# A windowed-attention and feed-forward kernel whose instructions are put in order by another simulator of the framework

## The chip, the cores and the metric

One core of a Trainium2 chip runs the kernel. The metric is the device time of one execution in microseconds (us); lower is better. Several runs of one kernel are summed up by their median. Engines are named as in the profile: PE is TensorE (matrix multiplies), PEld its weight loads, DVE is VectorE, ACT is ScalarE, POOL is GpSimd, and SP is the queue from which this kernel issues its DMA transfers.

## The reference

Attention over 8 batches and 8 heads, with 512 local and 32 global tokens a head and a head width of 64. Global queries see every key; local queries see the global keys and a window of 32 positions to each side. The result, 4352 rows of 512, goes through a feed-forward that takes the maximum of three products:

```python
s_g = scale * np.matmul(q_g, k_all.transpose(0, 1, 3, 2))
out_g = np.matmul(sm(s_g), v_all)
s_ll = np.where(np.abs(pos[:, None] - pos[None, :]) <= 32, scale * np.matmul(q_l, k_l.transpose(0, 1, 3, 2)), -1e9)
s_lg = scale * np.matmul(q_l, k_g.transpose(0, 1, 3, 2))
a_l = sm(np.concatenate([s_lg, s_ll], axis=-1))
out_l = np.matmul(a_l, np.concatenate([v_g, v_l], axis=2))
...
x = np.ascontiguousarray(attn_out.transpose(0, 2, 1, 3)).reshape(B * S, H * D)
h = np.maximum(np.maximum(x @ w1, x @ w2), x @ w3)
return (h @ w_out).astype(np.float32)
```

Everything is float32. `sm` is a softmax.

## The kernel before

**The work and its tiles.** Two heads make a pair (`p`), four pairs a batch, so there are 32 pairs. A pair's 512 local queries are cut into 4 items of 128 queries (`t`), which makes 128 items (`sl`). An item's keys are 192 or 224 columns: its window and the 32 global ones. Most operands are split into a high part, rounded to fp32r, and a low part, the rest, so that a product is made of two or three fast matmuls. The split is a `copy` (L101, on DVE or ACT) and a `sub` (L94, on DVE or POOL). The first 28 items take plain float32 instead of split q and k.

**An item's chain.** `scores` (L324) multiplies q and k into a PSUM tile `S`. DVE scales, masks and takes the maximum (L354), ACT takes the exponential (L356), DVE sums and inverts (L358, L359), `times` (L109) scales `s`, on POOL (L120), DVE or ACT, and from item 16 on SP stores `s` into `prob` (L363). `trans` (L367) transposes it on PE into the PSUM tile `T` (L375), from which `pt` is split. `transg` (L386) transposes the global queries' probabilities (L393), which `glob` (L278) and `glob_soft` (L302) have made from one block of scores in each of a pair's first two items (L290, L294). `pv` (L403) multiplies `pt` by v into the PSUM tile `O` (L419, L426), and ACT and DVE add its parts into `xr`.

**The feed-forward as a filler.** `moe_group` (L449) is a generator that emits one matmul at a time (L465 for the three products, L484 for the second layer). `fill(n)` takes n of them, so that between the small matmuls of an item there are always some of the batch before. From item 16 on the counts are (4, 4, 3, 7). The first batch's feed-forward starts at item 8. The last batch's, and that of the global rows, have no attention beside them and run at the end. Evictions of their PSUM tiles are a `copy` and running maxima on DVE (L473); `h` and `xs` are split like the rest.

**The front.** 24 pieces of weights arrive as float32 and are rounded and split on ACT, POOL and DVE by hand (`convert`, L150), in steps that lie between the items of the first batch (`weight_step`, L189; the table `WS`, L512).

**What sets the order.** The Python code writes instructions down in one order, for all engines together:

```python
trans(sl + 1)
fill(n[0])
next_scores(sl + 4 if sl < 12 else max(15, sl + 3))
...
fill(n[1])
pv(sl)
...
fill(n[2])
transg(sl + 1)
fill(n[3])
split_v(sl + 2)
load_v(sl + 4)
```

`next_scores` calls `scores`, then `split_q` for the item after, then `load_q`. Which engine an operation goes to is decided there too, by a running sum of estimated costs (`least`, L84). When the `TileContext` is left, the framework orders each engine's instructions by executing the program on a simulated machine: among the instructions whose inputs and tiles are ready there, the one written first goes next. It gives out the buffers of each pool in the same pass and then sets the semaphores. On the chip, each engine's and each queue's instructions come in the order found.

## Time and profile before

| | |
|---|---|
| median of 3 runs | 837.66 us (835.61 to 838.0) |
| profiled execution | 835.65 us, span 833.5 us |
| PE busy | 807.3 us, 97% of the span |
| DVE, ACT, POOL busy | 522.6, 528.3, 513.9 us (63%, 63%, 62%) |
| DMA | 93.56 MB by SP's queue |
| mean granted PE clock | 0.993 of full speed |

The profiled execution's own time is 2.15 us longer than its span, and it is one of the quicker runs. A busy time is the union of an engine's instructions. Matmuls overlap in the pipeline and their ends are modelled, so a full stretch of PE says that it always had work, not that it ran at its peak. Engine busy shares are averages over stages with different limits, so they are read stage by stage below.

### The profile page before, as it was taken

What the parts mean: (1) busy time and instruction counts of PE and PEld (TensorE: products, weight loads), DVE (VectorE), ACT (ScalarE), POOL (GpSimd) and SP (SyncE); (2) the same over time, 40 slices, a digit from 0 to 9 for tenths busy, and PEclk for the clock granted to TensorE, in tenths of its full rate; (3) what the DMA queues carried; (4) which work ended last, traced back from release to release, by engine and by line L of the source; (5) the groups of instructions that cost most, each with busy time, mean ns of one, the idle gap of its engine ahead of it and who ended that gap; (6) DMA issues with size and microseconds to landing.
All of it is one profiled execution on the core that took longest, in us unless ns stands there. A gap on an engine that the chain in (4) does not pass through costs nothing.

```text
span 833.5 us, 15973 instructions
## 1 busy us (share of the span) xinstructions
PE 807.3 (97%) x4668; PEld 684.4 (82%) x4668; DVE 522.6 (63%) x1784; ACT 528.3 (63%) x1498; POOL 513.9 (62%) x727
## 2 busy tenths in 40 slices
PE   7789899899999999999999999999999999999997
PEld 5569788878888888888888888888888888888896
DVE  4778735867776767767676776777776776411111
ACT  6688756776776777777776677777677666411210
POOL 4789836886677667867676676866776664311211
PEclk9899999999999999999999999999999999999999
DMA  7567544443334333343335333443335331100001
GB/s 261 175 225 228 183 127 131 137 130 103 105 115 143 114 91 112 105 146 100 103 106 166 107 99 109 120 140 94 95 93 172 109 90 53 59 13 1 26 26 26
DMA packets 93414, 94.56 MB, mean 113 GB/s; under 512 B 18448, under 2 KB 81808, under 8 KB 93328
## 3 DMA queue, kind: packets, MB, share of 16 engines
q1 hardware_dynamic: 93328, 93.56, 36.3%
q8 instruction: 37, 0.61, 0.3%
q14 instruction: 49, 0.40, 0.2%
HBM read 56.85 MB, written 8.91 MB: 79 GB/s over the span
## 4 chain that ended last, share of the span: by engine, by line
PE 83%; DVE 1%; POOL 1%; issue 1%; ACT 1%; DMA 0%; POOLq 0%; DVEq 0%; ACTq 0%
PE pm L465 48%; PE pm L484 16%; PE O L426 6%; PE S L351 5%; PE T L375 4%; PE S L294 2%; PE S L393 1%; PE S L347 1%; PE O L419 1%; DMA prob<-s 0%; ACT s L356 0%; DVE kst L105 0%; POOL s L120 0%; DVE xr L434 0%; DVE sg L298 0%
## 5 line engine op out<-in xcount | busy, mean ns | idle before, releaser
L465 PE MATMUL pm<-xs,wh 128*128 128x512 f32 (+1 forms) x1440 | 422.0, 368 | 5.7 <-ACT xs L107 2.3
L465 PEld LDWEIGHTS pm<-xs,wh 128*128 128x128 f32 x1440 | 253.3, 189 | 36.4 <-ACT xs L107 2.7
L465 PE MATMUL pm<-xs,wl 128*128 128x512 f32 (+1 forms) x720 | 265.1, 368 | 0.2 <-POOL wl L173 0.2
L465 PEld LDWEIGHTS pm<-xs,wl 128*128 128x128 f32 x720 | 136.3, 189 | 20.6 <-issue 1.6
L120 POOL TENSOR_SCALAR s<-s,z 128x224 f32<-128x224 f32 (+1 forms) x246 | 104.9, 438 | 64.8 <-ACT lox L107 40.9
L484 PE MATMUL pm<-woh,h 128*128 128x512 f32 x408 | 133.4, 399 | 0.9 <-POOL h L99 0.9
L99 POOL TENSOR_TENSOR h<-m,h 128x512 fp32r<-128x512 f32 (+1 forms) x60 | 68.6, 1143 | 97.8 <-ACT h L107 97.6
L356 ACT ACTIVATE s<-s,nm 128x224 f32<-128x224 f32 (+1 forms) x256 | 118.1, 462 | 16.5 <-DVE nm L354 12.8
L473 DVE TENSOR_TENSOR m<-pm,m 128x512 f32<-128x512 f32 (+1 forms) x120 | 73.0, 608 | 72.1 <-PE pm L465 71.6
L99 POOL TENSOR_TENSOR qs<-qraw,qs 128x256 fp32r<-128x256 f32 x100 | 73.1, 739 | 62.5 <-ACT qs L107 54.2
L99 DVE TENSOR_TENSOR pt<-T,pt 128x512 fp32r<-128x512 f32 x102 | 70.5, 691 | 62.6 <-ACT pt L107 61.3
L354 DVE CUSTOM_DVE_ANT_0 s<-S,mask 128x224 f32<-128x224 f32 (+1 forms) x240 | 80.7, 371 | 24.5 <-PE S L347 18.0
L484 PEld LDWEIGHTS pm<-woh,h 128*128 128x128 f32 x408 | 74.6, 188 | 13.6 <-POOL h L99 1.5
L484 PE MATMUL pm<-wol,h 128*128 128x512 f32 x204 | 82.1, 403 | 1.2 <-POOL wol L173 1.2
L99 POOL TENSOR_TENSOR kst<-kraw,kst 64x576 fp32r<-64x576 f32 x50 | 71.6, 1432 | 12.9 <-issue 6.2
L99 POOL TENSOR_TENSOR vs<-vraw,vs 128x256 fp32r<-128x256 f32 x102 | 75.4, 740 | 6.3 <-ACT vs L107 3.0
L107 ACT CAST pt<-T 128x512 fp32r<-128x512 f32 x88 | 51.3, 583 | 40.4 <-PE T L375 40.4
L107 ACT CAST qs<-qraw 128x256 fp32r<-128x256 f32 x99 | 40.2, 407 | 53.9 <-PE S L351 50.3
L426 PEld LDWEIGHTS O<-pt,vs 128*128 128x128 f32 x408 | 66.1, 188 | 8.8
L426 PE MATMUL O<-pt,vs 128*128 128x320 f32 (+1 forms) x408 | 72.8, 300 | 0.0
L351 PEld LDWEIGHTS S<-kst,qs 128*128 128x128 f32 x400 | 59.6, 190 | 8.9 <-DVE nmg L298 0.6
L434 DVE TENSOR_TENSOR xr<-O,lox 64x160 f32<-64x160 f32 x204 | 64.3, 315 | 3.4
(97 smaller groups left out, 1222.6 us busy)
## 6 DMA issues: line engine op xcount, KB each, us to landing
vraw<-v_in SPq DMA_DIRECT2D x64, 256.0 KB, 3.1
qraw<-q_in SPq DMA_DIRECT2D x100, 128.0 KB, 2.2
prob<-s SPq DMA_DIRECT2D x56, 224.0 KB, 2.4
wraw<-w_in SPq DMA_DIRECT2D x24, 512.0 KB, 3.6
prob<-s SPq DMA_DIRECT2D x56, 192.0 KB, 2.3
out_dram<-o SPq DMA_DIRECT2D x32, 256.0 KB, 2.5
kraw<-k_in SPq DMA_DIRECT2D x25, 320.0 KB, 3.0
qn<-q_in SPq DMA_DIRECT2D x8, 256.0 KB, 5.6
```

The lines of the kernel that those rows point to most:

```text
L99: (dve if least(c) == "d" else pool).tensor_tensor(out=out, in0=a, in1=b, op=ALU.subtract)
L107: act.copy(out=out, in_=a)
L120: pool.tensor_scalar(out=out, in0=a, scalar1=col, scalar2=1.0, op0=ALU.mult, op1=ALU.mult)
L351: pe.matmul(ph[j][:, 0:n], lhsT=qs[i][:, a, 128 * j:128 * j + 128], rhs=kst[p][:, j, c0:c0 + n], start=(a == 0), stop=(a == 1))
L354: dve.tensor_tensor_reduce(out=s[:, j, 0:n], in0=ph[j][:, 0:n], in1=mask[:, (1, 0, 1, 0)[t], 32 * (t == 0):32 * (t == 0) + n], scale=-0.12 ...
L356: act.activation(out=s[:, j, 0:n], in_=s[:, j, 0:n], func=AF.Exp, bias=nm[:, j:j + 1], scale=-1.0, accum_out=ze[:, j, 0:1])
L375: pe.transpose(pr[:, 256 * j + 128 * c:256 * j + 128 * c + 128], s[:, j, 128 * c:128 * c + 128], one)
L426: pe.matmul(o[:, j, 0:320].rearrange("p (a q) -> p a q", a=2)[:, :, 0:n], lhsT=vs[sl][:, 2 * j + c].rearrange("p a d -> p (a d)"), rhs=pt[ ...
L434: dve.tensor_tensor(out=xr[p][64 * j:64 * j + 64, t], in0=o[0:64, j, 0:160], in1=lo[:, j], op=ALU.add)
L465: pe.matmul(ps[:, 0:n], lhsT=w[f][:, i, k], rhs=xs[k][:, a, c0:c0 + n], start=(q == 0), stop=(q == 11))
L473: dve.tensor_tensor(out=m[:, 0:n], in0=ps[:, 0:n], in1=m[:, 0:n], op=ALU.max)
L484: pe.matmul(ps, lhsT=hh[f][:, a, 128 * t:128 * t + 128], rhs=w[:, f], start=(q == 0), stop=(q == 17))
```

## The change

One argument: the context is told to order the instructions by the framework's timeline simulation instead of its core simulation. The kernel's body stays as it is, and with it every instruction, the engine that it runs on, and every tile and transfer. What may differ is the place of an instruction in its engine's queue, the buffer that a tile gets, and the waits that follow from both.

```diff
-    with tile.TileContext(nc) as tc:
+    with tile.TileContext(nc, schedule_with_timeline_sim=True) as tc:
```

## The prediction

> **What bounds the kernel now.** I read the page first, then the busy time by stretches, then what TensorE (PE) waited for, then the chain of work that ended last, and only then single instructions. From the page:
>
> ```profile
> span 833.5 us, 15973 instructions
> ...
> PE 807.3 (97%) x4668; PEld 684.4 (82%) x4668; DVE 522.6 (63%) x1784; ACT 528.3 (63%) x1498; POOL 513.9 (62%) x727
> ...
> PE   7789899899999999999999999999999999999997
> ...
> PEclk9899999999999999999999999999999999999999
> ```
>
> PE is busy nearly throughout; what it lacks lies in the first slices. The stretches show it in numbers (after each engine its busy us, then PE's granted clock, DMA share, GB/s):
>
> ```profile
> 0.00:180.00 180.00, 158.54 (x1097) 132.02 (x1098) 121.22 (x440) 127.26 (x379) 127.93 (x197) 0.97 0.57 180
> 180.00:720.00 540.00, 540.00 (x2990) 458.17 (x2990) 381.39 (x1306) 382.72 (x1084) 369.61 (x514) 1.00 0.36 111
> 720.00:833.50 113.50, 108.80 (x585) 94.22 (x583) 20.01 (x38) 18.30 (x37) 16.32 (x17) 0.99 0.06 21
> ```
>
> ```profile
> 0.00:20.00 20.00, 14.92 (x73) 10.36 (x74) 9.06 (x55) 12.37 (x40) 9.21 (x24) 1.00 0.78 262
> 20.00:60.00 40.00, 30.67 (x184) 22.09 (x183) 30.47 (x103) 30.01 (x89) 30.77 (x50) 0.87 0.61 195
> 60.00:100.00 40.00, 37.39 (x293) 33.65 (x292) 33.37 (x92) 32.33 (x88) 36.38 (x49) 1.00 0.68 216
> 100.00:140.00 40.00, 39.41 (x300) 33.80 (x299) 17.93 (x86) 23.28 (x76) 19.14 (x30) 1.00 0.46 139
> 140.00:180.00 40.00, 36.14 (x257) 32.12 (x256) 30.38 (x110) 29.28 (x89) 32.43 (x47) 1.00 0.43 127
> ```
>
> There are three stages. In the front (0 to 180 us) PE is idle 180 - 158.54 = 21.46 us, and between 20 and 100 us DVE, ACT and POOL are as loaded as it is: weights are converted there beside the attention of the first batch. In the middle (180 to 720 us) PE has no idle time and the full clock, while the other three are busy 382.72 us of 540 at most, 71%. The tail (from 720 us) is the feed-forward of the last batch and of the global rows, with the others nearly idle; its 4.7 us without PE lie at the very end. So PE's amount of work is the bound, and only the front's 21.46 us stand above it. What PE waited for, over the whole run:
>
> ```profile
> PE S L290 <- DMA qg<-k_in: 4.2, 1, 4.2
> PE S L393 <- POOL probg L120: 2.3, 1, 2.3
> PE pm L465 <- ACT xs L107: 2.3, 2, 1.5
> PE pm L465 <- POOL xs L99: 2.2, 2, 1.8
> PE T L375 <- DMA prob<-s: 1.4, 3, 0.8
> ```
>
> The first is the first load, which no order can shorten. The others are single waits of 0.8 to 2.3 us, on three different engines: no one resource holds the front.
>
> **The change part by part.** It adds and removes no instruction, tile or transfer. It changes which simulated machine decides, instruction by instruction, what each engine and the DMA queue is given next; the chip then takes each queue in that order. So the whole price is a price of order, stage by stage. First, how far does the present order already depart from the written one? PE, from the chain of waits:
>
> ```profile
> 402.50 0.29 PE T L375 x4
> 402.79 1.00 PE pm L465 x4
> 403.79 0.44 PE S L351 x4
> 404.23 0.94 PE pm L465 x4
> 405.16 0.58 PE O L426 x4
> 405.75 0.70 PE pm L465 x3
> 406.44 0.06 PE S L393
> 406.50 1.67 PE pm L465 x7
> ```
>
> That is the order in which the loop writes it: transposes, 4 feed-forward matmuls, scores, 4, PV, 3, the global transpose, 7, the (4, 4, 3, 7) of L558. Here the simulated order made no choice on PE. On POOL it did:
>
> ```profile
> 404.75 0.74 POOL L99 TENSOR_TENSOR qs<-qraw,qs 128x256 fp32r<-128x256 f32 x1 [2.45 <-ACT qs L107]
> 406.29 0.88 POOL L120 TENSOR_SCALAR s<-s,z 128x224 f32<-128x224 f32 x2 [0.80 <-ACT lox L107]
> 407.14 0.74 POOL L99 TENSOR_TENSOR vs<-vraw,vs 128x256 fp32r<-128x256 f32 x1
> ```
>
> The loop writes the scaling of s (in scores) before the split of the next q (split_q), and here the split goes first. So POOL, and by the same reasoning ACT, DVE and the queue of SP, are the ones to be reshuffled.
>
> Middle, 540 us: I cost it at 0. A gain is excluded: PE has no idle time there. What hides a reshuffle is the slack of the other engines. The tightest hand-over I find is the PSUM tile S, of which there are two: in an item with a global score block, the tile of S L351 has to be read by DVE before the global transpose (L393) can be given it, if the two take turns.
>
> ```profile
> 410.21 0.35 DVE L354 CUSTOM_DVE_ANT_0 s<-S,mask 128x192 f32<-128x192 f32 x1
> ```
>
> ```profile
> 412.24 0.22 PE L393 MATMUL S<-identr,probg 128*128 128x128 f32 x1
> ```
>
> DVE is done at 410.56, PE needs the tile at 412.24: 1.68 us of slack. The longest DVE operation that could step ahead is the running maximum:
>
> ```profile
> 404.89 0.69 DVE L473 TENSOR_TENSOR m<-pm,m 128x512 f32<-128x512 f32 x1
> ```
>
> Two of these (1.38 us) still fit; three (2.07 us) cost 0.39 us an item. That cover gone, over the 54 items behind the front that have such a block (t of 0 or 1, pairs 4 to 30), is 0.39 x 54 = 21 us: the upper end for this stage. Long waits elsewhere are no sign of danger:
>
> ```profile
> POOL h L99 <- ACT h L107: 97.6, 27, 18.4
> ...
> SPq L363 <- POOL s L120: 189.6, 74, 8.6
> ```
>
> The first row is POOL standing with h at the head of its queue. What is behind it there (scalings of s, splits of q and v) waits too, and PE does not notice. The second is SP standing with the store of s into prob, with the loads of q and v behind it; PE lost only the 1.4 us of its row above to that hand-over. If the new order puts a load of q ahead of a prob store, or the reverse, SP pays with time it has.
>
> Tail, 113.5 us: 0, since PE alone fills it, and 4.7 us are the last eviction and store.
>
> Front: this is where an order has something to win or lose. Upper end of a gain: 21.46 less the first load's 4.2, so 17 us, plus what the clock costs there. The granted clock by short stretches:
>
> ```profile
> 22.00:24.00 2.00, 0.26 (x1) 0.18 (x1) 1.97 (x5) 0.60 (x2) 1.82 (x5) 0.82 0.85 247
> 24.00:26.00 2.00, 2.00 (x9) 1.28 (x9) 0.52 (x4) 0.62 (x1) 1.82 (x6) 0.50 0.44 118
> 26.00:28.00 2.00, 2.00 (x14) 1.44 (x13) 1.95 (x7) 0.95 (x3) 1.16 (x1) 0.82 0.41 162
> ```
>
> A stretch with almost no matmul is followed by one at half the clock. It costs 2 x 0.50 + 2 x 0.18 = 1.4 us of PE; the mean of 0.87 over 20 to 60 us means 40 x 0.13 = 5 us in all. So the gain ends at 22 us. For a loss I take the same 22 us as the end, a front with twice the waits. Between these ends I stay near zero, nearest to the rows of single waits (0.8 to 2.3 us): a new order would remove some and make others. I lean to +1.5 us, less than one wait of 2.3, because the stretch with the most matmuls per us among the loaded ones, 60 to 100 us, has only 2.6 us of PE idle left to win and POOL busy 36.38 of 40 us: one operation in the wrong place there has nothing to hide behind.
>
> [...]
>
> Sum: 835.65 us is the time of the profiled execution (span 833.5 and 2.15 around it); + 0 (middle) + 0 (tail) + 1.5 (front) = 837.2. The median of the runs, 837.66, is 2.0 above the profiled one, so against it I say 839.
>
> **The rivals.**
> 1. The front gets better: the other machine places conversions, scalings and splits closer to when their inputs are really there, and a third to two thirds of the 22 us go, 7 to 15. For it: the PE waits there fall on single late operations (xs, probg), which one place earlier would cure. Against it: ACT, DVE and POOL are busy 75 to 91% between 20 and 100 us, so the room is small, and I take the lower half: 837.66 - 9 = 829, and 823 at the best.
> 2. The middle loses its cover: DVE or POOL is given the feed-forward's evictions ahead of the reading of S by three operations or more in every such item. For it: the period repeats, so that a bad place is paid 54 times. Against it: 29% of slack on each engine, and PE's own order has not moved at all there. Price as above: 837.66 + 21 = 859; it decides from 1.7 us of delay on.
> 3. The clock: the front's waits stay as long in sum but fall so that two or three more stretches run at half the clock, 3 x 1.4 = 4.2 us, with the 1.5 of the front 843 us. For it: three 2 us stretches of the kind above fit into the 5 us found. Against it: it can as well lose one.
> 4. Nothing moves that PE sees, because both machines find PE the bound: 837.7.
>
> **How the numbers follow.** A measurement of this kernel tells 0.3% from no change, 2.5 us: same is 835.1 to 840.2. My forecast (front shifted by a few us, middle untouched) has 0.50, with its own range 834 to 845: 0.08 of that is faster, 0.23 same, 0.19 slower. Rival 1 has 0.19, all faster; rival 2 0.18, slower; rival 3 0.05, slower; rival 4 0.08, same. Faster 0.08 + 0.19 = 0.27; same 0.23 + 0.08 = 0.31; slower 0.19 + 0.18 + 0.05 = 0.42. The range leaves out the better half of rival 1 (below 828) and the worse half of rival 2 (above 857, where the delay passes 1.68 us by more than 0.36 in each of 54 items): about 0.19 together.
>
> **What would show it.** Right: PE still fully busy from 180 to 720 us at the period of before, its idle time differing only ahead of 180 us, by under 5 us, and POOL's order of qs, s and vs changed. The middle's step is wrong if PE shows waits there at S (L393, L351) or T (L375), or if its row of items no longer reads T, 4, S, 4, O, 3, S, 7. The front's step is wrong if PE idles under 15 or over 28 us before 180 us. The whole is wrong if the new order moves PE itself: feed-forward matmuls pulled ahead in the front would then be missing as filler later, a cost that no row here prices.

## The result and the profile after

The changed kernel takes 894.89 us (median of 4 runs, 891.57 to 896.84) against 837.14 us for the one before: a ratio of 1.0696, 95% interval 1.0678 to 1.0714, so 7% slower. I had said 839 us, with 857 as the upper end. The profiled execution took 893.29 us, with a span of 891.5 us and a mean granted clock of 0.955. One execution among the experiments below (of frontload_spare) took 939.16 us at a mean granted clock of 0.849, and no comparison uses it.

The page of the changed kernel, its span, busy times, PE's busy tenths in 40 slices and its granted clock:

```profile
span 891.5 us, 15955 instructions
...
PE 833.7 (94%) x4668; PEld 710.1 (80%) x4668; DVE 501.6 (56%) x1784; ACT 521.3 (58%) x1498; POOL 513.8 (58%) x727
...
PE   7688999989998999989999999979998999979997
...
PEclk9979999999998899979999999979998899989999
```

PE has the same 4668 matmuls, yet is busy 26.4 us longer (833.7 against 807.3), and idle 57.8 us instead of 26.2 (span less busy): together the 58 us of longer span. The slices show where: there are dents at regular distances, a busy 7 or 8, most of them with a clock of 7 or 8. Before, both rows were flat there. The same stretches as in the prediction:

```profile
0.00:180.00 180.00, 154.93 (x1064) 130.09 (x1065) 116.56 (x415) 119.12 (x358) 121.98 (x188) 0.95 0.54 173
...
180.00:720.00 540.00, 518.53 (x2746) 442.26 (x2745) 333.23 (x1216) 351.57 (x1011) 347.91 (x483) 0.95 0.34 106
```

The front lost little: 25.1 us idle instead of 21.5. The middle, which had none, has 21.5 us of idle time, a clock of 0.95, and gets through 2746 matmuls where it had done 2990.

One dent in the busy time by 2 us (columns as before: PE, PEld, DVE, ACT, POOL, granted clock, DMA share, GB/s):

```profile
380.00:382.00 2.00, 1.88 (x16) 1.62 (x14) 1.02 (x4) 1.50 (x5) 1.09 (x3) 1.00 0.37 122
382.00:384.00 2.00, 0.83 (x7) 0.73 (x7) 2.00 (x9) 1.79 (x8) 1.55 (x3) 1.00 0.71 210
384.00:386.00 2.00, 1.31 (x9) 0.86 (x8) 1.31 (x8) 1.31 (x5) 1.28 (x3) 0.77 0.17 39
386.00:388.00 2.00, 1.37 (x6) 1.16 (x7) 1.72 (x6) 1.95 (x6) 1.75 (x4) 0.50 0.22 67
388.00:390.00 2.00, 2.00 (x9) 1.90 (x10) 1.25 (x7) 1.93 (x7) 1.85 (x3) 0.50 1.01 275
390.00:392.00 2.00, 0.90 (x6) 0.74 (x6) 1.82 (x7) 0.97 (x4) 1.90 (x3) 0.50 0.53 165
392.00:394.00 2.00, 2.00 (x10) 1.90 (x10) 2.00 (x7) 1.95 (x6) 2.00 (x4) 0.50 0.31 97
```

PE has some work in each 2 us, but too little in most, and from 386 to 394 us it runs at half the clock. The chain of the same place (start, us, what; the shorter pieces left out):

```profile
379.86 0.47 PE pm L465 x2
...
380.72 0.67 PE O L426 x4
...
383.11 0.80 DVE pt L99 x2
...
385.00 0.60 ACT s L356 x3
...
388.48 2.64 DMA qraw<-q_in
...
391.57 1.30 PE O L426 x4
392.87 0.80 PE S L351 x4
393.67 1.33 PE pm L465 x3
```

And a little later:

```profile
399.56 5.26 PE pm L465 x23
...
407.65 2.80 PE pm L465 x12
...
415.64 3.50 PE pm L465 x15
```

Read against the row of 4, 4, 3, 7 of before, this shows what was lost in the middle. From 380.3 to 393.7 us there is no feed-forward matmul (L465); the end of the chain walks through DVE, ACT, POOL and a load instead of through PE. Behind it the feed-forward matmuls come in packs of 23, 12 and 15. Counts of L465 and of the PV matmuls (L426; 4 to an item) in two stretches of one batch, before first:

```profile
300.00:336.00 36.00, 30.23 (x112) 19.26 (x112) 1.00 0.35 104
384.00:396.00 12.00, 9.90 (x38) 6.36 (x37) 1.00 0.26 79
```

```profile
300.00:336.00 36.00, 4.58 (x27) 4.40 (x28) 1.00 0.35 104
384.00:396.00 12.00, 1.42 (x8) 1.30 (x8) 1.00 0.26 79
```

The changed kernel, L465 and then L426:

```profile
300.00:336.00 36.00, 29.57 (x124) 22.10 (x123) 1.00 0.29 87
384.00:396.00 12.00, 1.53 (x3) 0.88 (x3) 0.57 0.49 140
```

```profile
300.00:336.00 36.00, 3.71 (x20) 3.02 (x20) 1.00 0.29 87
384.00:396.00 12.00, 3.97 (x14) 2.97 (x15) 0.57 0.49 140
```

Early in the batch 124 matmuls of filler now go with 20 of PV, 25 an item (124 / 20 x 4); before it was 112 with 27, 17 an item. At the batch's end 3 go with 14, less than one an item, where 38 went with 8. A batch's filler is fixed, so what goes early is missing late. The next batch's filler cannot step in: each of its products sums over the four pairs of a batch (L463), so it waits for the attention of the last pair. From 372.3 us on, ahead of the dent, 27 of its matmuls have gone already, which fits nine, those of three pairs, in each of the three PSUM tiles `pm`. The dents come about every 100 us (the first near 188, the last near 786 us, six periods), where a batch took 92.4 before.

### The profile page after: what moved, and what is told of

It is laid out like the page before. It is cut to its first block, busy times and chain, and to the rows that moved or that the text cites. A ratio compares the mean times of both kernels' runs of the same rounds, so it can differ in the third digit from the quotient of the medians.

```text
span 891.5 us, 15955 instructions
## 1 busy us (share of the span) xinstructions
PE 833.7 (94%) x4668; PEld 710.1 (80%) x4668; DVE 501.6 (56%) x1784; ACT 521.3 (58%) x1498; POOL 513.8 (58%) x727
## 4 chain that ended last, share of the span: by engine, by line
PE 84%; DVE 4%; DMA 4%; ACT 3%; issue 2%; POOL 1%; SPq 1%; ACTq 0%; DVEq 0%; POOLq 0%
PE pm L465 48%; PE pm L484 15%; PE O L426 7%; PE S L351 5%; PE T L375 4%; PE S L347 2%; PE S L294 1%; PE O L419 1%; DMA wraw<-w_in 1%; DMA prob<-s 1%; ACT s L356 1%; PE S L393 1%; DVE s L354 1%; DMA probg<-sg 1%; DVE xr L434 1%
## 5 line engine op out<-in xcount | busy, mean ns | idle before, releaser
L465 PE MATMUL pm<-xs,wh 128*128 128x512 f32 (+1 forms) x1440 | 413.0, 369 | 6.6 <-ACT m L107 3.1
L465 PEld LDWEIGHTS pm<-xs,wh 128*128 128x128 f32 x1440 | 261.1, 194 | 46.0 <-ACT xs L107 3.7
L465 PE MATMUL pm<-xs,wl 128*128 128x512 f32 (+1 forms) x720 | 263.0, 366 | 0.0
L465 PEld LDWEIGHTS pm<-xs,wl 128*128 128x128 f32 x720 | 139.2, 193 | 20.0 <-POOL wct L161 0.6
L484 PE MATMUL pm<-woh,h 128*128 128x512 f32 x408 | 129.4, 394 | 0.0
L426 PE MATMUL O<-pt,vs 128*128 128x320 f32 (+1 forms) x408 | 83.0, 328 | 11.2 <-DVE xr L434 9.8
L107 ACT CAST h<-m 128x512 fp32r<-128x512 f32 (+1 forms) x60 | 33.4, 556 | 93.1 <-DVE m L473 93.0
L484 PEld LDWEIGHTS pm<-woh,h 128*128 128x128 f32 x408 | 75.2, 188 | 15.0 <-DVE nm L354 0.6
L107 ACT COPY lox<-O 64x320 f32<-64x320 f32 x100 | 42.3, 423 | 74.5 <-PE O L426 73.7
L484 PE MATMUL pm<-wol,h 128*128 128x512 f32 x204 | 79.8, 396 | 0.0
L426 PEld LDWEIGHTS O<-pt,vs 128*128 128x128 f32 x408 | 66.3, 202 | 16.5 <-POOL s L120 4.5
L351 PE MATMUL S<-kst,qs 128*128 128x192 f32 (+1 forms) x400 | 72.2, 294 | 5.0 <-DVE nm L354 4.6
L432 DVE TENSOR_TENSOR lox<-O,lox 64x320 f32<-64x320 f32 x102 | 48.9, 480 | 48.1 <-ACT lox L107 47.2
```

Of the source, the lines that this page charges most:

```text
L107: act.copy(out=out, in_=a)
L351: pe.matmul(ph[j][:, 0:n], lhsT=qs[i][:, a, 128 * j:128 * j + 128], rhs=kst[p][:, j, c0:c0 + n], start=(a == 0), stop=(a == 1))
L426: pe.matmul(o[:, j, 0:320].rearrange("p (a q) -> p a q", a=2)[:, :, 0:n], lhsT=vs[sl][:, 2 * j + c].rearrange("p a d -> p (a d)"), rhs=pt[ ...
L432: dve.tensor_tensor(out=lo, in0=o[0:64, :, 160:320], in1=lo, op=ALU.add)
L465: pe.matmul(ps[:, 0:n], lhsT=w[f][:, i, k], rhs=xs[k][:, a, c0:c0 + n], start=(q == 0), stop=(q == 11))
L484: pe.matmul(ps, lhsT=hh[f][:, a, 128 * t:128 * t + 128], rhs=w[:, f], start=(q == 0), stop=(q == 17))
```

## Experiments

In all of them the names are those of the two kernels. "Pinned" means that an engine's instructions are kept in the written order, by a wrapper round the engine:

```diff
+    class InOrder:
...
+                i = f(*a, **k)
+                return tc.keep_in_program_order(i) if pinned[0] else i
...
+    pe = InOrder()
...
+        pinned[0] = sl >= 16
```

The simulation then places everything else anew around the pinned engine, so the queues of the others need not be those of the kernel that the run starts from.

### Only PE put back: pin16

The changed kernel with PE pinned from item 16 on, as in the diff above.

> The timeline simulation orders everything, but from item 16 on each PE instruction is held behind the one written before it. Theory A (PE's own order, which pulls the feed-forward matmuls ahead and leaves the last items of a batch without filler, is the cause): the middle is back at 92.4 us a batch with no idle PE, and the time is 842 us (835 to 850), what is left above 837 being the front. Rival B (the new order of DVE, ACT, POOL and SP is the cause, PE's order only follows): PE still waits in the middle, 870 to 895 us.

Measured: 859.48 us, ratio to before 1.0293 [1.0262, 1.0324], between the two ranges. Its front and middle, and an item of the middle:

```profile
0.00:180.00 180.00, 146.98 (x991) 121.79 (x991) 111.87 (x391) 114.69 (x340) 112.74 (x174) 0.92 0.52 167
180.00:720.00 540.00, 534.92 (x2964) 452.78 (x2965) 378.79 (x1307) 382.24 (x1084) 372.23 (x520) 1.00 0.36 112
```

```profile
401.83 1.00 PE pm L65 x4
402.83 0.44 PE S L65 x4
403.26 0.94 PE pm L65 x4
404.20 0.58 PE O L65 x4
404.78 0.70 PE pm L65 x3
405.48 0.06 PE S L65
405.54 1.67 PE pm L65 x7
```

(L65 is the wrapper.) With only PE held to the written order the clock of the middle is 1.00 again and the dents are gone. Of the 5.1 us that PE idles in the second row 2.6 lie ahead of 200 us, so the other engines' new order costs little behind. That recovers 35 of the 58 us. Some 23 us stay. They lie in the main ahead of 200 us: PE is idle 33.0 us there to 180 us instead of 21.5, at a clock of 0.92 instead of 0.97.

### PE's order made by hand, without the other simulation: frontload

The kernel before (core simulation), PE pinned from item 16, and the filler counts written so that a batch's filler goes early:

```diff
+        if sl >= 32:
+            n = {0: (0, 0, 0, 0), 1: (3, 3, 2, 4), 13: (4, 3, 3, 5), 14: (0, 0, 0, 0), 15: (0, 0, 0, 0)}.get(sl % 16, (6, 5, 4, 9))
```

> The core simulation of the kernel before, PE held to the written order from item 16 on, and the filler of each batch from item 32 on written early by hand, as the changed kernel has it: about 24 matmuls in each of 11 items, then 15, 0, 0, and 0 and 12 in the first two of the next batch. Theory A: six lulls at batch ends, each some 7 us, with PE idle and at half the clock in them: 877 us (865 to 890). Rival B (filler placement harmless): 837 to 842 us.

Measured: 902.45 us, 1.0793 [1.0756, 1.083]. It is more than I expected, even longer than the changed kernel, with the same kind of dents (20 us of one are shown below) and with nearly the front of before (23.7 us idle to 180 us). Pinning does not make the dents: in core_pin0 below, which has the core simulation and PE pinned throughout, but the filler spread as before, the middle is full:

```profile
180.00:720.00 540.00, 539.10 (x2983) 456.60 (x2982) 382.89 (x1316) 383.49 (x1088) 371.82 (x518) 1.00 0.37 113
```

So gathering the filler is enough to make a loss of this kind, also when the core simulation orders the rest.

### What the clock has to do with it: frontload_warm and frontload_spare

A dent costs idle time and half clock. To part the two, PE was given work that no result needs. In frontload_warm each matmul of T, of S in `scores` and of O is issued twice in the items without filler:

> As frontload, but in the items without filler every transpose, score and PV matmul is issued twice (the same result again, about 1.7 us of PE more an item, some 25 us in all). Theory C (a good part of a lull is lost to the half clock, which sparse matmuls bring on): the lulls run at a higher clock and the added work costs less than nothing, 10 us below frontload or so (frontload minus 20 to minus 3). Rival D (a lull is set by the chain of DVE, ACT, POOL and DMA, and the clock does not matter): 0 to 25 us above frontload.

Measured: 909.9 us, 1.0882 [1.0845, 1.0919], 7 us more than frontload and in rival D's range. In the middle PE is idle 25.3 us instead of frontload's 35.9 and the clock is 0.97 instead of 0.95, but it still fell to 0.50 in the dents. The second matmuls stand in the chain of attention itself, so the run changes the length of the chain along with the clock and does not part the two.

In frontload_spare the added work is independent of attention: 8 matmuls of 512 columns in each of 20 items, whose product nothing reads.

```diff
+    def extra(n):
+        if n:
+            ps = pm.tile([128, 512], F32, name="pm")
+            for _ in range(n):
+                pe.matmul(ps, lhsT=wh[0][:, 0, 0], rhs=wo[0][:, 0], start=True, stop=True)
...
+        spare = (2, 2, 1, 3) if sl >= 30 and sl % 16 in (14, 15, 0) else (0, 0, 0, 0)
```

> As frontload, but 8 more matmuls of 512 columns (into a spare feed-forward tile whose result is not used) stand in each item without filler, where filler would stand: about 130 in all, 30 us of PE at full clock. They are in nobody's chain. Theory C (the half clock takes a good part of each lull, since it doubles the PE steps of the attention chain): the lulls run at full clock and the time falls below frontload in spite of the added work, 885 to 900 us. Rival D (the lull is as long as the chain of the other engines, at whatever clock): 902 to 925 us.

Measured: 891.7 us (890.77 to 893.53), 1.0669 [1.0647, 1.069], 11 us less than frontload although PE has more to do. The profile comes from a second run of the same kernel, frontload_spare_b:

> The same kernel as frontload_spare, once more for its profile: frontload with 8 independent matmuls of 512 columns, whose product nothing reads, in each item that has no filler left. Theory C (the clock's part of the loss comes from PE being too empty in the lulls): in the lulls the granted clock stays at 0.9 or more where frontload showed about 0.5, and the mean is 0.97 or more against frontload's 0.957; time 885 to 900 us. Rival D (the lulls are latency alone): the clock in the lulls stays near 0.5 and the mean below 0.96.

Measured: 889.2 us (one run). A dent of frontload and the same stretch of frontload_spare_b:

```profile
376.00:396.00 20.00, 12.40 (x70) 10.38 (x70) 15.64 (x56) 14.34 (x43) 13.69 (x20) 0.81 0.45 144
```

```profile
376.00:396.00 20.00, 17.82 (x101) 14.13 (x100) 14.70 (x61) 15.99 (x50) 15.06 (x22) 1.00 0.50 158
```

The clock stays at 1.00 there, and over the whole middle, in the same order:

```profile
180.00:720.00 540.00, 504.13 (x2663) 424.16 (x2662) 333.02 (x1177) 344.81 (x976) 335.73 (x468) 0.95 0.34 104
```

```profile
180.00:720.00 540.00, 529.21 (x2868) 441.81 (x2867) 338.65 (x1200) 351.46 (x996) 344.10 (x478) 1.00 0.34 105
```

The balance: PE is busy 849.1 us in all, 13.9 more than frontload's 835.2, and idle 38.3 instead of 66.9. The 160 added matmuls take about 38 us at the 0.24 us that the row of seven L465 gives (1.67 / 7), so by this estimate the needed work takes 849.1 - 38 = 811 us, near the 807.3 of before; in frontload the same work took 835.2. The half clock was thus worth some 24 us there, and it came from PE being too empty. The two spans differ by less, 902.1 - 887.4 = 14.7 us: 24 less for the clock, 38 more for the added work, 28.6 less idle, since most of the added work fell into holes. Even so the kernel stays 53 to 55 us above before.

### The front: pin0 and core_pin0

PE pinned from the first instruction on, once with the timeline simulation, once with the core simulation.

> As pin16, but PE is held to the written order from the first instruction. Theory A: the middle as in pin16; the front differs by what the freedom of PE's order is worth in the first 16 items, some single waits of 1 to 2 us: 845 us (836 to 856). Rival B: 870 to 895 us.

> The core simulation, with PE held to the written order from the first instruction: beside pin0 the only change is the order of DVE, ACT, POOL and SP. Theory E (what is left of the loss in the front comes from the order of these engines, above all from weight conversions placed behind the attention): 845 us (840 to 852), PE's freedom in the first items being worth the 9 us that pin0 lost to pin16. Rival F (it comes from PE's order in the first items): 860 to 870 us, like pin0.

Measured: 868.64 us, 1.039 [1.0371, 1.0409], and 847.23 us, 1.013 [1.0114, 1.0147]. The first lies between its two ranges, the second in theory E's. PE's order is the same written one in both, so the 21 us between them are the price of what the timeline simulation does to ACT, DVE, POOL and SP and to the buffers given out. PE's own freedom is worth 9 us in the first 16 items with the one (868.6 against pin16's 859.5) and 11 us over the whole run with the other (847.2 against 836.5).

### Late weights: load_twice and ws_early

In the changed kernel and in pin16 the weights are late. The last step of a weight's conversion on DVE (ns, first and last start), of before, pin16 and after:

```profile
L167 DVE SCALAR_TENSOR_TENSOR wct<-wraw,W x24: 669/680/689, 23.4 to 101.8; 128x512 int32<-128x512 int32 x24
```

```profile
L179 DVE SCALAR_TENSOR_TENSOR wct<-wraw,W x24: 670/686/689, 18.9 to 115.8; 128x512 int32<-128x512 int32 x24
```

```profile
L167 DVE SCALAR_TENSOR_TENSOR wct<-wraw,W x24: 670/686/690, 18.9 to 131.7; 128x512 int32<-128x512 int32 x24
```

load_twice makes them late on purpose, in the kernel before:

```diff
         nc.sync.dma_start(out=r, in_=win[m])
+        nc.sync.dma_start(out=r, in_=win[m])
```

> The kernel before (core simulation, PE unpinned), with the DMA of every 24 weight pieces issued twice into the same tile, so that each piece arrives about one DMA time (some 5 us) later and SP's queue has 24 entries more. It adds 12.6 MB of DMA in the front and changes nothing behind it. Theory G (what the other front order costs is the lateness of the weights: first-layer and second-layer matmuls can't fill PE before their pieces are converted, and whatever ends the conversions later than the 101.8 us of before costs a good part of that lateness): the last conversion starts at 110 to 125 us and the time is 845 to 862 us, with PE's added idle time all ahead of 160 us. Rival H (the front's loss in the other order comes from attention operations being shuffled, the weights' lateness only goes along with it): 836 to 841 us although the conversions end later. The middle keeps its 92.4 us period in both.

Measured: 862.98 us, 1.031 [1.0289, 1.0331], 1 us above theory G's range. The delay was not 5 us, as I had written (in the kernel before, a piece landed 3.1 to 8.1 us after its issue, median 3.6), but grew from piece to piece:

```profile
L168 DVE SCALAR_TENSOR_TENSOR wct<-wraw,W x24: 674/682/687, 27.0 to 141.8; 128x512 int32<-128x512 int32 x24
```

40 us later than before, for 26.7 us of time. What PE waited for ahead of 200 us shows the weights at the top:

```profile
PE pm L466 <- POOL wl L174: 6.8, 7, 2.4
PE pm L466 <- ACT wh L171: 6.6, 3, 3.2
```

So late weights do cost, about 0.67 us for each us (26.7 / 40), an upper figure since the second loads also burden the queue. If the price is proportional, the 14 us of lateness in pin16 (115.8 against 101.8) come to 9 of its 23 us.

The waits of pin16 ahead of 200 us show another way in which a weight holds PE up. PE's longest sum, then ACT's:

```profile
PE pm L65 <- ACT m L119: 9.0, 3, 4.2
```

```profile
ACT wct L170 <- DMA wraw<-w_in: 14.1, 11, 3.1
```

The first is PE waiting for ACT to empty a feed-forward tile (the copy into `m`). Before two of the three waits ACT stands with a conversion at the head of its queue, whose weight has not arrived, and the copy stands behind it:

```profile
98.74 0.66 ACT L170 ACTIVATE wct<-wraw 128x512 f32<-128x512 f32 x1 [1.78 <-DMA wraw<-w_in]
99.30 0.36 ACT L119 COPY m<-pm 128x256 f32<-128x256 f32 x1
```

```profile
99.71 0.80 PE L65 MATMUL pm<-xs,wh 128*128 128x256 f32 x2 [4.18 <-ACT m L119]
```

PE's waits for converted weights themselves come to 3.9 us there. load_twice, where they lead, has the lateness without this order, so its rate need not hold for pin16.

ws_early goes the other way, in the kernel before:

```diff
-    WS = [1, 1, 2, 1, 2, 2, 1, 2] + [2] * 8 + [1] * 2
+    WS = [2, 2, 2, 2, 2, 2, 2, 2, 2] + [2] * 6 + [1] * 2
```

> The kernel before with one table changed: WS = [2]*9 + [2]*6 + [1]*2 in place of [1, 1, 2, 1, 2, 2, 1, 2] + [2]*8 + [1]*2, so that the conversion steps are written down 4 steps earlier in the first items. Theory G: the last conversion starts some us ahead of 101.8 us and the time is 830 to 836 us (the same or slightly faster than before). Rival H (conversions crowd out the attention of the first batch on ACT, DVE and POOL, which are 75 to 91% busy there): 838 to 845 us, with PE waiting on attention operations (S, T, O) ahead of 100 us. The middle is untouched in both.

Measured: 841.7 us, 1.0058 [1.0037, 1.0079], in the rival's range. The last conversion started at 101.2 us instead of 101.8: writing the steps earlier does not end them earlier, but their other places among the attention of the first batch cost 5 us. That is a price of places and not of a later end; three operations also went to DVE instead of ACT and POOL (1787 on DVE instead of 1784).

### Which engine's front order: one at a time

pin16, with one or more engines also pinned in the first 16 items (`front[0] = sl < 16`).

> As pin16, but in the first 16 items ACT, DVE and POOL are held to the written order too, so that weight conversions cannot fall behind later attention work. Theory E: most of the front's 23 us comes back, 838 to 850 us. Rival F (the transfers or PE's order of the first items make the loss): 857 us or more.

> pin16 (timeline order, PE in written order from item 16 on: 859.5 us, 23 us above before, all of it ahead of 200 us), with SP's queue also held to the written order in the first 16 items. Theory J (the weights come late because their loads stand in SP's queue behind stores and loads that wait; ACT waits 14.1 us for wraw in pin16 and 2.3 before): wraw is issued last at 93 to 98 us instead of 108.9, the conversions end by 105 and the time is 842 to 852 us. Rival K (the loads are late because the engines free their three buffers late, so SP's order does not matter): 856 to 866 us, wraw still last issued beyond 105 us.

> pin16 with ACT alone held to the written order in the first 16 items. If the front's loss lies in ACT's order: 842 to 852 us. If it lies elsewhere: 856 to 870 us. All three of ACT, DVE and POOL in written order gave 891, so at least one of them gets worse by it: the one that does stands above 870.

> pin16 with DVE alone held to the written order in the first 16 items. If the front's loss lies in DVE's order (its conversion steps of 2 us each put between the reads of S): 842 to 852 us. If it lies elsewhere: 856 to 870 us; above 870 if it is what made the version with all three engines in written order slow.

> pin16 with POOL alone held to the written order in the first 16 items. If the front's loss lies in POOL's order: 842 to 852 us. If it lies elsewhere: 856 to 870 us; above 870 if it is what made the version with all three engines in written order slow (there DVE's z held up POOL's scaling of s for 33.0 us).

| pinned in the first 16 items, beside pin16 | median us | ratio to before | last wraw load issued, us |
|---|---|---|---|
| nothing (pin16) | 859.48 | 1.0293 [1.0262, 1.0324] | 108.9 |
| POOL | 856.19 | 1.0234 [1.021, 1.0257] | 100.4 |
| SP | 866.26 | 1.0348 [1.0329, 1.0366] | 113.1 |
| ACT | 870.04 | 1.0395 [1.0375, 1.0414] | 109.9 |
| DVE | 880.34 | 1.0521 [1.0501, 1.0541] | 120.5 |
| ACT, DVE and POOL | 891.14 | 1.0654 [1.0636, 1.0672] | 130.0 |

Putting one queue into the written order wins 3 us (POOL) or loses 7 to 21; all three of ACT, DVE and POOL lose 32. No run came into the range that its theory had given for a loss in that queue. Theory J's forecast failed with the rest, since SP in written order issues the last weight at 113.1 us, later still; the run therefore does not say what early weights would win. The written order is not what the core simulation makes of these engines, so none of these runs clears a queue. What I can show of the front is that the orders of ACT, DVE, POOL and SP together are worth 21 us (pin0 against core_pin0), and that PE's waits for the copy into `m` are 9.0 us of pin16's front. How the rest divides stays open; the order of the core simulation, imposed on one engine under the other simulation, was not tried. Open too is why the timeline simulation finds the attention matmuls late and so lets the filler pass them.

## Why the prediction was wrong

**Which step failed: "Middle, 540 us: I cost it at 0."** It rested on "Here the simulated order made no choice on PE". That was read rightly from the chain, but it says only that the core simulation left the written order of PE alone. It does not say that another machine would. The timeline simulation did not: by the rule that the first ready instruction goes next, an attention matmul that is not ready there lets the next matmul of filler pass, and the batch runs out of filler. (The order is seen, 25 fillers an item and then less than one; the readiness is inferred, since the simulation's own times are not on record.) In place of 0 the middle took 21.5 us of idle time and ran at a clock of 0.95, and pin16, which undoes this, wins 35 us. I named this at the end ("feed-forward matmuls pulled ahead in the front would then be missing as filler later, a cost that no row here prices"), but for the front only, and gave it no chance. In the middle it repeats with every batch. pin16 and frontload show it from both sides. My sign for it, "The whole is wrong if the new order moves PE itself", came true.

**"A gain is excluded: PE has no idle time there"** held, and misled. An engine that is full for 540 us could only lose; its fullness was made by the even spread of the filler, and I took it for granted.

**The tile S (rival 2).** The mechanism did not come, although its sign, waits at S in the middle, did. PE waited for DVE's reading of S at L351, over the whole run, as little as the second row here says (us in total, times, longest):

```profile
PE O L426 <- DVE xr L434: 9.8, 11, 1.8
PE S L351 <- DVE nm L354: 4.6, 4, 1.3
```

They are short waits in the dents, where attention stands alone, and not one in each of 54 items.

**The front, +1.5 us.** Mis-sized. In pin16, where PE cannot make up for it later, the new order of the front costs 23 us, at the end of loss that I had set (22) and far from the value I took. I had taken each new wait for one more of 0.8 to 2.3 us; there the waits behind the copy into `m` alone come to 9.0 us, with 4.2 the longest. In the changed kernel the idle time ahead of 180 us rose by only 3.6 us, because PE filled the holes: by then it had done 509 feed-forward matmuls (L465 and L484), against 512 before, but only 224 PV matmuls against 236, three items fewer. So my mark for the front (idle between 15 and 28 us) was met, at 25.1, but with filler that the attention still to come then lacked.

**The clock (rival 3).** The right kind of cost in the wrong place and size. I priced a stretch at half the clock at 1.4 us and put two or three of them into the front. In the middle the dent above stays at 0.50 for 8 us (386 to 394), after 4 us in which PE was busy 0.83 and 1.31 of 2 us. PE's busy time grew by 26.4 us with the same matmuls, close to the 24 that frontload_spare_b gives for the half clock in frontload. So nearly half of the loss is clock, by these two estimates.

**The tail** stayed at its cost: apart from the last dent, which reaches into it, PE fills it as before.

## What to carry to other kernels

Where one engine is full only because an independent filler is spread evenly between the links of a latency-bound chain, the spread is itself the resource: ask of any change to the ordering whether the filler can run ahead, count fillers per item along a whole batch, and look at the item where they run out. A scheduler that always takes what is ready will spend the filler early if its model finds the chain slower than the other model did; pinning the full engine to the written order in that stretch is a cheap guard (35 of 58 us here; pinned in the front too it lost 9). "This engine's order has not moved so far" is a statement about the model that made it, not about the next one.

## What the runs showed of the hardware

In these runs the granted clock fell where PE was thinly supplied, without a long stop: in the changed kernel it went to 0.50 in dents behind waits of 1.8 us at most, and 8 added matmuls of 512 columns an item, whose product nothing reads, held it at 1.00 and made a kernel with some 38 us more work 11 us faster (891.7 against 902.45). Doubling matmuls within the waiting chain (frontload_warm) did not hold it: 0.97 over the middle, 0.50 in the dents.

How long it stayed down is in the windows of the changed kernel: in six of its seven dents it stood at 0.50, for 7 to 14 us each (487.6 to 494.2 us is one of the shortest, 282.8 to 296.2 one of the longest). The first dent kept it at 1.00 although PE was busy only 1.82 of 4 us there (188 to 192), less than the 2.42 of 4 just ahead of the fall in the third (381 to 385). What decides when it falls, these runs do not show.
